# A PSUM bank for VectorE's score tiles, zero products in TensorE's gaps, and the later tiles' Q deferred

## The chip, the cores and the metric

The kernel runs on one core of a Trainium2 chip. The metric is the device time of one execution in microseconds (us). All numbers below are medians of several executions unless a single profiled one is named.

## The reference, cut to what matters

Two blocks, each an attention layer and a feed-forward layer (FFN), on 2048 positions of width 512, in bf16. There are 32 heads of only 16 columns, so the score matrix has 32 x 2048 x 2048 entries for each attention layer, and each needs an exponential.

```python
def _A_ref(x, wqkv, wo):
    H = 32; Dh = D // H                      # B, S, D = 1, 2048, 512
    qkv = ((x @ wqkv).reshape(B, S, 3, H, Dh)).transpose(2, 0, 3, 1, 4)
    q, k, v = qkv[0], qkv[1], qkv[2]
    p = softmax(einsum("bhqd,bhkd->bhqk", q, k) * Dh ** -0.5)
    o = einsum("bhqk,bhkd->bhqd", p, v)
    return o.transpose(0, 2, 1, 3).reshape(B, S, D) @ wo
def _B_ref(x, w1, b1, w2, b2):
    return gelu(_layernorm(x) @ w1 + b1) @ w2 + b2       # 512 -> 1376 -> 512
x = x + _A_ref(_layernorm(x), ...);  x = x + _B_ref(x, ...)      # twice
```

(The first lines are condensed; the layer norm inside `_B_ref` has no weights.)

## The kernel before

Scores are made in tiles of 128 keys x 512 queries of one head: 4096 tiles in all, each filling one of the eight PSUM banks (`ps` is declared as 128 x 8 x 512 floats). ScalarE takes the exponential of most tiles, two or three banks in one instruction. VectorE takes some (448 before) by an arithmetic of its own: it copies the tile out as integers (`dt`), and then four instructions on a pair of tiles make the exponential (`de`). TensorE then multiplies the result by V into bank 6.

The order of each engine's instructions is fixed in advance. The program plays the run through with a duration written beside every instruction, takes on each engine the task with the best priority among those ready, and emits the instructions in that order. So these durations do not set the time on the chip, but they decide who stands behind whom, and which tiles VectorE gets (it takes one if the plan says it is nearly idle).

```python
while pos < len(seq):                              # flow_scores: all tiles, in order
    ...
    G = 3 if wide else 2                           # 2 only in the first part of layer 1
    grp = seq[pos:pos + G]
    ...
    r = gi % 2
    b0 = G * r                                     # banks 0-2, then 3-5, in turn
    yield ("keys", [... ("free", last[b]) ...])    # both readers must have finished
    pt = yield ("get", "pt")
    dpos = self.choose_d(grp)                      # 0: VectorE gets the first tile; None: it gets none
    ops = []                                       # the group's score products
    ...
    yield Task("pe", 0.0, ops)
    ...                                            # one exponential on the other 2 or 3 banks:
    S_.submit(Task("act", ..., [I(lambda e, ...: e.activation(out=self.PT[:, pt, k0:k0 + n, :],
              in_=self.ps[:, b0 + k0:b0 + k0 + n, :], func=ACTF.Exp, scale=EXPS), ..., 0.085 + 0.4267 * n)]), cb=...)
    if dpos is not None:                           # VectorE drains its bank of the same group
        S_.submit(Task("dve", 0.0, [I(lambda e, ...: e.tensor_scalar(out=self.dt32[...],
                  in0=self.ps[:, b, :], ...), [("ps", b)], [("dt", ds, w)], 0.61)]), cb=...)
```

Layer 1 (the first attention layer) starts on little data: its first 512 queries meet the first 512 keys ("first part"), and later the other 1536 keys ("second part"), which can begin when K and V of the other twelve tiles of 128 positions are there. For each tile one job does the layer norm, a transposing DMA (`xnT`), the projections to K, Q and V, the copies out of PSUM, and the stores.

```python
def job_qkv_tile(self, L, tt, slot, i, left, prio):
    xr = yield ("get", "xn")                       # 3 slots; held until the transpose has landed
    yield self.ln_apply(tt, slot, i, xnr, ("xn", xr), prio)
    xs = yield ("get", "xnT")
    yield self.dma(lambda e: e.dma_start_transpose(self.xnT[:, xs, :, :], xnr), ...)
    ...                                            # mm(1): K, mm(0): Q, mm(2): V; four products each
```

At the end of each part, VectorE turns a row of Q into a column to put the two parts together (`rowT`).

## Time and profile before

| | before |
|---|---|
| time, median of 3 (lowest, highest) | 2046.51 us (2046.08, 2049.51) |
| span of the profiled execution | 2049.5 us |
| ScalarE busy, of it in 1387 exponentials | 1760.0 us, 1690.9 us |
| ScalarE idle just before exponentials | 207.3 us |
| of it from 53 to 205 us, and later | 73.1 us, 134.2 us |
| mean clock granted to TensorE | 0.689 |

To read it: ScalarE's work sets the time, so its idle time before exponentials is what a change can win. The main lines stand in the prediction. Three more views are needed afterwards for comparison. First the score products in the costliest groups (busy, mean ns of one, idle before them and what ended it):

```profile
L849 PE MATMUL ps<-QT,KT 32*128 32x512 bf16 x4096 | 738.0, 515 | 231.9 <-ACT PT L862 215.4 <-ACT dw L1019 5.2 <-DVE QT L792 4.6
```

Next the table of waits of TensorE's weight loads (total us, times, longest): score products that stood until VectorE had drained its tile.

```profile
PEld ps L849 <- DVE dt L874: 47.2, 134, 1.3
```

And the two longest unbroken runs of exponentials in the chain that ended last, from 1300 us on (start, us, what):

```profile
1427.91 11.40 ACT PT L862 x9
...
1836.59 11.78 ACT PT L862 x9
```

A product takes 515 ns in the mean.

### The profile page before, as it was taken

The numbers are of one execution on the slowest core, as the hardware profiler recorded it, in microseconds if no ns is written. First come the engines' busy times: TensorE is split into PE (matmuls) and PEld (weight loads), VectorE is DVE, ScalarE is ACT, GpSimd is POOL, SyncE is SP. The second block draws the span as 40 slices with busy tenths as digits, with TensorE's granted clock in tenths as the row PEclk, the third lists the DMA queues.
The fourth block names the chain that finished last, engine by engine and source line by source line (L and its number), as shares of the span: only waits on it lengthen the run. The fifth ranks groups of instructions, "written<-read, shape, count | busy, mean of one in ns | idle before, by whom it ended". The sixth has DMA issues, their size and how long they took to land.

```text
span 2049.5 us, 24833 instructions
## 1 busy us (share of the span) xinstructions
PE 1622.3 (79%) x9544; PEld 387.5 (19%) x9544; DVE 1543.8 (75%) x2378; ACT 1760.0 (86%) x1452; POOL 111.0 (5%) x230
## 2 busy tenths in 40 slices
PE   2877888887888878878788777787788788887886
PEld 1211111221111211222112211122112221122112
DVE  4657656888789788879777875698788787797882
ACT  1744999897999889989899879999999899999992
POOL 4110000001100020000200010000000000000000
PEclk9775555896667775688658885579556875588557
DMA  7782000101000010001511142100000000000000
GB/s 186 91 83 42 17 11 14 16 3 47 25 5 16 21 50 6 16 3 27 118 29 21 12 50 37 30 16 14 6 6 10 9 17 6 6 16 14 1 1 21
DMA packets 177957, 57.33 MB, mean 28 GB/s; under 512 B 160593, under 2 KB 171698, under 8 KB 177842
## 3 DMA queue, kind: packets, MB, share of 16 engines
q1 hardware_dynamic: 177842, 55.74, 15.2%
q8 instruction: 79, 1.29, 0.3%
q14 instruction: 36, 0.29, 0.1%
HBM read 10.92 MB, written 17.53 MB: 14 GB/s over the span
## 4 chain that ended last, share of the span: by engine, by line
ACT 40%; PE 34%; DVE 17%; DMA 5%; issue 2%; POOL 2%; SPq 0%; POOLq 0%; DVEq 0%
ACT PT L862 37%; PE ps L849 12%; PE ps L968 9%; PE ps L685 4%; DVE dt L874 3%; PE ps L1080 3%; PE ps L1114 3%; PE ps L1048 3%; DVE de L927 2%; DMA xnT<-xn 2%; DVE accT L998 2%; ACT h L1107 2%; DVE h L1100 1%; DVE de L930 1%; DVE dv L928 1%
## 5 line engine op out<-in xcount | busy, mean ns | idle before, releaser
L862 ACT ACTIVATE PT<-ps 128x1536 bf16<-128x1536 f32 (+1 forms) x1387 | 1690.9, 1308 | 207.3 <-PE ps L849 198.0
L849 PE MATMUL ps<-QT,KT 32*128 32x512 bf16 x4096 | 738.0, 515 | 231.9 <-ACT PT L862 215.4
L968 PE MATMUL ps<-PT,V 128*17 128x512 bf16 x3648 | 570.2, 515 | 38.4 <-DVE accT L998 19.7
L874 DVE TENSOR_SCALAR dt<-ps 128x512 int32<-128x512 f32 x448 | 299.9, 682 | 258.7 <-PE ps L849 257.6
L849 PEld LDWEIGHTS ps<-QT,KT 32*128 32x128 bf16 x4096 | 167.6, 96 | 835.4 <-PE ps L849 446.1
L927 DVE SCALAR_TENSOR_TENSOR de<-dt 128x1024 bf16<-128x1024 uint16 x226 | 270.2, 1199 | 1.4
L930 DVE SCALAR_TENSOR_TENSOR de<-dt,dv 128x1024 uint16<-128x1024 int32 x226 | 269.2, 1206 | 1.5
L685 PE MATMUL ps<-wqkv,xnT 128*128 128x512 bf16 x384 | 135.8, 475 | 72.7 <-DMA xnT<-xn 46.4
L968 PEld LDWEIGHTS ps<-PT,V 128*17 128x17 bf16 x3648 | 105.4, 89 | 406.0 <-issue 302.3
L968 PE MATMUL ps<-de,V 128*17 128x512 bf16 x448 | 140.9, 525 | 19.0 <-DVE de L930 19.0
L929 DVE TENSOR_TENSOR dv<-de,dv 128x1024 f16<-128x1024 bf16 x226 | 149.5, 675 | 0.2
L928 DVE TENSOR_SCALAR dv<-dt 128x1024 bf16<-128x1024 uint16 x226 | 149.4, 675 | 0.0
L1080 PE MATMUL ps<-yT,w 128*128 128x512 bf16 (+1 forms) x352 | 108.3, 421 | 25.0 <-DMA yT<-xn 13.2
L1114 PE MATMUL ps<-w,h 128*128 128x512 bf16 x280 | 86.8, 436 | 20.3 <-ACT g L1108 16.6
L998 DVE STREAM_TRANSPOSE accT<-ps 128x512 f32<-128x512 f32 x80 | 56.7, 708 | 55.8 <-PE ps L968 55.7
L637 POOL TENSOR_SCALAR rs<-mv 128x4 f32<-128x4 f32 (+1 forms) x19 | 11.6, 611 | 1601.6 <-DVE mv L630 1601.3
L1048 PE MATMUL ps<-wo,OT 128*128 128x512 bf16 x256 | 77.2, 422 | 3.3 <-DVE xres L1050 2.6
L1100 DVE TENSOR_SCALAR h<-ps,b1c 128x512 f32<-128x512 f32 (+1 forms) x77 | 56.7, 736 | 12.6 <-PE ps L1080 12.2
L685 PEld LDWEIGHTS ps<-wqkv,xnT 128*128 128x128 bf16 x384 | 31.1, 108 | 141.7 <-issue 73.9
L1031 DVE STREAM_TRANSPOSE OT<-ob 128x512 bf16<-128x512 bf16 x64 | 45.0, 702 | 0.3
L629 DVE BATCH_NORM_STATS2 st<-xres 128x6 f32<-128x512 bf16 x64 | 42.5, 669 | 0.0
L1080 PEld LDWEIGHTS ps<-yT,w 128*128 128x128 bf16 (+1 forms) x352 | 27.7, 104 | 76.4 <-issue 35.6
(94 smaller groups left out, 610.5 us busy)
## 6 DMA issues: line engine op xcount, KB each, us to landing
q_scr<-qk SPq DMA_DIRECT2D x22, 256.0 KB, 2.1
k_scr<-qk SPq DMA_DIRECT2D x12, 256.0 KB, 2.0
q_scr<-h SPq DMA_DIRECT2D x10, 256.0 KB, 3.8
m_scr<-accT SPq DMA_DIRECT2D x16, 136.0 KB, 9.2
MA<-m_scr SPq DMA_DIRECT2D x16, 136.0 KB, 2.2
out_dram<-xres SPq DMA_DIRECT2D x16, 128.0 KB, 1.7
v_scr<-vst SPq DMA_DIRECT2D x12, 136.0 KB, 1.7
V<-v_scr SPq DMA_DIRECT2D x8, 204.0 KB, 4.6
```

The source lines that it names most:

```text
L685: yield Task("pe", prio, [I(lambda e, c=c: e.matmul(self.ps[:, b, :], lhsT=self.xnT[:, xs, c, :], rhs=self.wqkv[:, c, which * 512:which * ...
L849: ops.append(I(lambda e, hp=hp, hg=hg, kb=kb, q=q, b=b: e.matmul(self.ps[:, b, :], lhsT=self.KT[32 * hp:32 * hp + 32, hg, kb * 128:(kb + 1 ...
L862: S_.submit(Task("act", 0.0 + 1e-5 * gi, [I(lambda e, pt=pt, k0=k0, n=n, b0=b0: e.activation(out=self.PT[:, pt, k0:k0 + n, :], in_=self.ps ...
L874: S_.submit(Task("dve", 0.0, [I(lambda e, ds=ds, w=w, b=b: e.tensor_scalar(out=self.dt32[:, ds, w * 512:(w + 1) * 512], in0=self.ps[:, b, ...
L927: yield Task("dve", pr, [I(lambda e: e.scalar_tensor_tensor(out=E, in0=lo, scalar=65536.0, in1=lo, op0=ALU.subtract, op1=ALU.mult), RT, [( ...
L928: yield Task("dve", pr, [I(lambda e: e.tensor_scalar(out=v, in0=lo, scalar1=CUB_B * sc / 65536.0, scalar2=CUB_A * sc, op0=ALU.mult, op1=AL ...
L929: yield Task("dve", pr, [I(lambda e: e.tensor_tensor(out=D, in0=E, in1=v, op=ALU.mult), [("de", es), ("dv", s)], [("dv", s)], 0.06 + 0.521 ...
L930: yield Task("dve", pr, [I(lambda e: e.scalar_tensor_tensor(out=Pb, in0=t32, scalar=2.0 ** -9, in1=D, op0=ALU.mult, op1=ALU.subtract), RT ...
L968: ops.append(I(lambda e, hp=hp, hg=hg, kb=kb, ap=ap, first=first: e.matmul(self.ps[32 * hp:32 * hp + 17, ACCB, :], lhsT=self.V[:, hg, kb, ...
L1048: yield Task("pe", pr, [I(lambda e, hg=hg, i=i, b=b: e.matmul(self.ps[:, b, :], lhsT=self.OT[:, hg, i * 128:(i + 1) * 128], rhs=self.wo[:, ...
L1080: yield Task("pe", pr, [I(lambda e, c=c: e.matmul(self.ps[0:M, b, :], lhsT=self.w1[:, c, fc * 128:fc * 128 + M], rhs=self.yT[:, c, :], sta ...
L1114: yield Task("pe", pr, [I(lambda e, fc=fc, i=i, b=b: e.matmul(self.ps[:, b, :], lhsT=self.gt(fc, i), rhs=self.w2[:, fc, :], start=(fc == 0 ...
```

## The change

Its intent has three parts. VectorE's tiles get bank 5 for themselves, and ScalarE works on groups of three tiles (banks 0 to 2) and two (banks 3 and 4) in turn, so that no group waits for two readers. Where the plan sees TensorE idle for more than 0.35 us, products with a zero matrix are put in, to keep its clock up; they add zero to bank 6, or write zeros to bank 7 while it is free. And Q of the later twelve tiles is left out at the start and made when K and V are done. With it the planned durations were set anew, and on-chip memory was found for a thirteenth slot of `PT` and the zero matrix: `rowT` lost its own buffer and takes one of the three `xn` slots. The new layout brought smaller rules with it: VectorE may take a tile from the next head group too, it stops 16 tiles before the end of a head group instead of 14, and value products wait for fewer ready tiles (5 instead of 9).

```diff
+            if t.eng == "pe" and self.filler is not None:      # in the scheduler
+                gap = pick[0] - self.P.free["pe"]
+                if gap > FILL_GAP:                             # 0.35
+                    self.filler(gap)
...
+    def fill_pe(self, gap):
+        n = int(FILL_F * (gap - 0.15) / FILL_T)                # 0.8, 0.11
+        ...
+        for _ in range(n):
+            P.op("pe", lambda e: e.matmul(self.ps[:, b, 0:FILL_N], lhsT=self.zw[:, :], rhs=self.wqkv[:, 0, 0:FILL_N], start=st, stop=st, skip_group_check=True), ...)
...
-            G = 3 if wide else 2
+            if wide:
+                b0, G = ((0, 3), (3, 2))[gi % 2]
+            else:
+                b0, G = ((0, 2), (2, 2))[gi % 2]
...
+            dt = self.take_d() if wide else None               # a tile for VectorE, into bank DLANE = 5
...
-        self.PT = t("PT", [128, PT_GROUPS, 3, 512], BF16)
+        self.PT = t("PT", [128, 13, 512], BF16)
-        self.rowT = t("rowT", [128, 512], BF16)
...
-            yield Task("dve", 1.2, [I(lambda e: e.transpose(self.rowT[:, :], self.QT[:, q, :]), [("qt", q)], [("rowT",)], 0.6)])
+            xs = yield ("get", "xn")
+            RX = ("xn", xs)
+            yield Task("dve", 1.2, [I(lambda e: e.transpose(self.xn[:, xs, :], self.QT[:, q, :]), [("qt", q)], [RX], 0.68)])
...
+        if later is not None:                                  # job_lnqkv: first "kv", then "q"
+            yield ("keys", [("n2k", L, tt) for tt in range(self.NT)])
+            for i, tt in enumerate(tiles):
+                self.S_.spawn(self.job_qkv_tile(L, tt, slot, i, left, later + 0.01 * i, "q"), later + 0.01 * i)
...
+LAT_PE = 0.20                                                  # planned: from a product to its reader (0.13 before)
...                                                            # and most planned durations, such as:
-  [("ps", b)], [("dt", ds, w)], 0.61)
+  [("ps", DLANE)], [("dt", ds, w)], 0.66)
```

In the program's order this makes 701 exponentials of three tiles, 764 of two and one of one, against 874 and 513; 464 tiles for VectorE against 448; and 3574 zero products.

## The prediction

> **What bounds the kernel now.** I read first the table of busy shares and the strip of slices, then the costliest groups, then the waits of ScalarE stretch by stretch, then a timeline of one plain attention stretch.
>
> ```profile
> PE 1622.3 (79%) x9544; PEld 387.5 (19%) x9544; DVE 1543.8 (75%) x2378; ACT 1760.0 (86%) x1452; POOL 111.0 (5%) x230
> ...
> ACT  1744999897999889989899879999999899999992
> ...
> PEclk9775555896667775688658885579556875588557
> ...
> L862 ACT ACTIVATE PT<-ps 128x1536 bf16<-128x1536 f32 (+1 forms) x1387 | 1690.9, 1308 | 207.3 <-PE ps L849 198.0
> ```
>
> ScalarE sets the time. It is busy 1760 us, nearly all of it in the 1387 exponentials, and the third number of the last line is the point: 207.3 us of idle stand just before those exponentials, of which 198.0 end when a score product lands. The rest of the 2049.5 us is a head (the first exponential starts at 53.3 us) and a tail (the last one starts at 2001.2 us). So with the same ScalarE work the most that can be won is about 207 us. PE's 79% is no bound: a product waiting in the pipe counts as busy. The clock row shows that TensorE is at half clock for long stretches.
>
> Where do the 207 us lie? The same ScalarE groups, by shape, in three stretches (each block is headed by its columns in the view; busy and mean of one, then idle before):
>
> ```profile
> L862 ACT ACTIVATE PT<-ps 128x1024 bf16<-128x1024 f32 x75 | 73.9, 1024 | 72.4 <-PE ps L849 71.6
> ...
> L862 ACT ACTIVATE PT<-ps 128x1536 bf16<-128x1536 f32 x368 | 505.1, 1467 | 26.3 <-PE ps L849 25.1
> L862 ACT ACTIVATE PT<-ps 128x1024 bf16<-128x1024 f32 x197 | 198.0, 1033 | 49.3 <-PE ps L849 46.8
> ...
> L862 ACT ACTIVATE PT<-ps 128x1536 bf16<-128x1536 f32 x333 | 455.2, 1465 | 14.5 <-PE ps L849 13.4
> L862 ACT ACTIVATE PT<-ps 128x1024 bf16<-128x1024 f32 x192 | 192.4, 1038 | 23.8 <-PE ps L849 20.8
> ```
>
> The first line is 53 to 205 us (start of layer 1), the next two 350 to 1150, the last two 1300 to 2001. The start alone loses 73 us. In the two long stretches the short exponentials (two tiles, because VectorE took the third) lose 49.3/197 = 0.25 and 23.8/192 = 0.12 us each, the long ones only 26.3/368 = 0.07 and 14.5/333 = 0.04. The remaining 21 us are 3.6 between 205 and 350 and 17 at the change of layers (1150 to 1300). So the mixed groups are what hurts, as the change supposes.
>
> ```profile
> 53.00:205.00 152.00, 117.61 (x524) 25.70 (x520) 95.32 (x185) 87.14 (x85) 21.73 (x67) 0.66 0.64 71
> ...
> 1440.00:1550.00 110.00, 54.20 (x264) 11.56 (x261) 0.50 0.03 6
> ...
> 1478.21 0.14 PEld L849 LDWEIGHTS ps<-QT,KT 32*128 32x128 bf16 x3 [0.67 <-PE ps L849]
> 1478.24 0.61 PE L849 MATMUL ps<-QT,KT 32*128 32x512 bf16 x3 [0.19 <-ACT PT L862]
> ```
>
> The first line is the start in the table of stretches: ScalarE busy 87 of 152 us, DMA share 0.64, no engine full; it is a chain of transfers, projections and evictions. The second is the score products in a stretch without projections: 264 of them and a clock of exactly 0.50. The last two show a refill there: three products take 0.61 us at half clock and wait for ScalarE to leave the banks.
>
> **What the Trainium skill says.** "TensorE: Matmul & The Clock Gate", Part 1: the array runs at half clock unless the last activity window of about 3.4 us was busy, and the granted ratio is binary. The trace agrees (0.50 held for whole stretches) and adds something: score and value products, which use 32-row or 32-column tiles, do not count enough. Between 1440 and 1550 us PE is issuing all the time and stays at 0.50, while stretches with full 128x128 projections reach 0.75 to 0.93. "PSUM — Partial Sum Buffer", section on bank collisions: two engines may not touch one bank and quadrant together, so a bank goes back to TensorE only when its reader has finished; here the three banks of a group go back only when both ScalarE and VectorE are done. "TensorEngine Tiling (Array Packing)", Key Properties: changing the tiling mode drains TensorE. The trace shows 0.23 us of weight-load wait at warm switches, so fillers (full mode) between tiled products are not free. "ScalarE: Activation LUTs", What ACT_TABLE_LOAD costs: back-to-back activations overlap by some 93 ns. Here two of 1024 take 1.94 us and one 1.03, so 0.92 each; eleven of 1536 take 14.77 in the chain of waits and one 1.45, so 1.33 each.
>
> **The change part by part.** Counts are from the built programs' instruction order.
>
> ScalarE work. Before: 874 long and 513 short exponentials, 874 x 1.33 + 513 x 0.92 = 1634 us. After: 701 long, 764 short and one of a single tile (0.5): 932 + 703 + 1 = 1636 us. Gelu and table loads are the same. VectorE takes 464 tiles in place of 448, which just pays for the 79 extra instructions. Net +2 us: the change does not unload ScalarE, it can only remove idle.
>
> VectorE's own bank. Before, after a short exponential ScalarE has only 0.92 us of cover while TensorE refills three banks, one of which VectorE has first to drain (0.68 us, and it may stand behind a 1.2 us instruction). After, ScalarE's groups wait for ScalarE alone. But the cover alternates for good: the two-bank group is refilled under 1.33 us, the three-bank group under 0.92 us, some 690 times. A refill is a release of about 0.19 us, products of 0.61 (cold) or 0.39 (warm), and about 0.1 to the start of the activation: 0.9 cold, 0.68 warm. Cold it has no slack; warm it has 0.24 us. So this part needs the next one.
>
> Zero products. 3574 products of 256 columns in some 760 bursts. By columns they equal 1787 full products; TensorE has 1344 of its own. Counted along the order, every run of 64 scores has at least 31 full-product equivalents, or at least 3.6 per 3.4 us at 7.5 scores per window. Laying the clock record over the products before, windows that stayed warm had mostly 3 or more full ones (mean 5.7) and windows that stayed cold 0.4. So I expect the clock at 0.9 or above from 60 us on. Their cost: at full clock 256 columns are half of the 0.215 us seen for a warm 512-column projection, so 3574 x 0.107 = 382 us plus 760 switches x 0.1 = 76. The other PE work when warm: 1466 score groups x 0.32 = 469, some 1200 value groups x 0.32 = 384, 1344 x 0.215 = 289 and switches about 50. Sum 1650 us in 1950: it fits, but PE has little slack, and a burst placed wrongly holds a score group by up to some 0.5 us.
>
> Mid-kernel sum. Idle before exponentials from 205 to 2001 us is 134 now. After: in stretches without projections, half of the 690 cycles, warm slack of 0.24 us leaves perhaps 0.02 each (7 us); in stretches with projection and FFN pairs of 0.53 us, which cannot be interrupted, I take the 0.12 us that warm three-tile groups after two short ones wait now (345 x 0.12 = 41); layer change 15. About 65. Gain 134 - 65 = 69 us.
>
> Early Q deferred. For 12 tiles, Q projection (4 products at 0.43, 20 us in all when cold), a VectorE eviction, half of the square and its sum and one small operation (0.69 + 0.34 + 0.6 + 0.18, 22 us in all) and the 256 KB store (landing about 4 us in this stretch) leave the start; later 12 more normalisations (0.40 each) and 12 input transposes come back at low priority, where the DMA share is 0.06. The first part of layer 1 has 64 short exponentials: 64 x 0.92 = 59, so it could end at 112 us, but the second part starts at 179 because K and V of 12 tiles are late. The load of that stretch falls by roughly a quarter on PE, VectorE and DMA, so 118 us (60 to 178) become about 88. Gain about 30 us, leaving some 43 of the 73.
>
> Sum: 2046.5 + 2 - 69 - 30 = 1950 us, after rounding.
>
> **The rivals.** (a) PE becomes the bound: the fillers run late, or the clock stays cold and each takes 0.21 us. Against it: cold overfull PE is itself activity that warms the clock, and the sum above leaves 300 us. For it: an order fixed in advance, and every score group sits behind whatever is in front. It would leave mid idle near 134 or above, time 1990 to 2060. (b) The start is bound by transposes, which stay (KT and xnT land in about 5.4 us, DMA share 0.77 to 0.80 in slices up to 150): deferral gains 10 rather than 30, time 1970. (c) VectorE becomes the bound: 28 half batches instead of 4 and 16 more tiles add about 50 us to 1544, so 82% of 1950; in FFN stretches it is at 88% now. Time 1970 to 1980. (d) Everything aligns: mid idle 30, start idle 25, time 1900.
>
> **Range and chances.** Main uncertainty is the mid term (gain 20 to 100) and the start (10 to 45), largely independent: 1905 to 2000 for 8 in 10. 2% is 41 us, that is below 2005.6; only rival (a) or two halved terms together miss it. Faster 0.88, within 0.11, slower 0.01.
>
> **What would show it.** Clock row at 8 to 9 nearly throughout; ScalarE busy within 20 us of 1760; idle before its exponentials near 110 instead of 207, with the long ones now waiting more than the short; second part of layer 1 starting near 150 instead of 179; no wait of scores on VectorE's drain of any size. Wrong if the clock stays near 0.7, if idle before exponentials remains above 170, or if score products are found standing behind zero products.

## The result, and the profile after

The changed kernel takes **1915.39 us** (median of 4, 1911.82 to 1917.96), a ratio of 0.9351 with a 95% interval of 0.9332 to 0.9370. Ratios here are the mean time of one kernel's runs over that of the other's runs of the same rounds, so they are not quite the ratio of the medians quoted. That is faster, inside the predicted range, and 35 us below the predicted 1950.

The page of the changed kernel: busy shares, the strip of the clock, and two of the costliest groups.

```profile
span 1913.1 us, 32397 instructions
...
PE 1743.7 (91%) x13118; PEld 671.1 (35%) x13118; DVE 1600.0 (84%) x2511; ACT 1734.6 (91%) x1531; POOL 122.2 (6%) x230
...
PEclk9989999999999999999999989999999999999999
...
L921 ACT ACTIVATE PT<-ps 128x1024 bf16<-128x1024 f32 (+1 forms) x1466 | 1666.1, 1293 | 100.4 <-PE ps L915 96.3
...
L853 PE MATMUL ps<-wqkv,zw 128*128 128x256 bf16 x3574 | 530.0, 277 | 0.0
```

The clock row is at 8 or 9 throughout, and the idle before exponentials is 100.4 us instead of 207.3. There are also 25 us less of busy time in them, though ScalarE has 79 more instructions to do; that is taken up below. By stretch (53 to 205 us, 350 to 1150, from 1300), as the prediction shows it of before:

```profile
L921 ACT ACTIVATE PT<-ps 128x1024 bf16<-128x1024 f32 x89 | 89.8, 1055 | 33.7 <-PE ps L915 33.3
...
L921 ACT ACTIVATE PT<-ps 128x1536 bf16<-128x1536 f32 x321 | 482.4, 1503 | 17.8 <-PE ps L915 16.2
L921 ACT ACTIVATE PT<-ps 128x1024 bf16<-128x1024 f32 x320 | 344.7, 1077 | 17.8 <-PE ps L915 17.5
...
L921 ACT ACTIVATE PT<-ps 128x1536 bf16<-128x1536 f32 x235 | 362.1, 1541 | 4.2 <-PE ps L915 3.0
L921 ACT ACTIVATE PT<-ps 128x1024 bf16<-128x1024 f32 x234 | 261.1, 1116 | 4.7 <-PE ps L915 4.6
```

The start loses 33.7 us (with 6.0 before long exponentials, 39.7) instead of 73.1. Long and short groups now wait alike: 0.06 us each in the middle, 0.02 in the last stretch. The table of stretches for 53 to 205 and 205 to 350 us (busy us and instructions of PE, PEld, DVE, ACT, POOL, then clock, DMA share, GB/s):

```profile
53.00:205.00 152.00, 128.09 (x863) 43.75 (x860) 110.86 (x218) 119.63 (x117) 17.84 (x27) 0.93 0.61 66
205.00:350.00 145.00, 129.76 (x1000) 49.58 (x999) 130.03 (x227) 133.17 (x123) 14.06 (x35) 0.96 0.12 32
```

At the start ScalarE is busy for 119.63 of 152 us instead of 87.14. The timeline of TensorE in a quiet stretch shows what the refills look like now:

```profile
1474.36 0.39 PE L915 MATMUL ps<-QT,KT 32*128 32x512 bf16 x3 [0.19 <-ACT PT L921]
1474.69 0.39 PE L1040 MATMUL ps<-PT,V 128*17 128x512 bf16 x4
...
1475.93 0.61 PE L853 MATMUL ps<-wqkv,zw 128*128 128x256 bf16 x4
1476.62 0.39 PE L915 MATMUL ps<-QT,KT 32*128 32x512 bf16 x3
```

Three score products take 0.39 us, where they took 0.61. The four zero products take 0.61 together, of which the first is 0.27, so about 0.11 for each further one, and the scores after them follow. Over the whole kernel the score products show the same (group list, with the idle before them):

```profile
L915 PE MATMUL ps<-QT,KT 32*128 32x512 bf16 x4096 | 600.3, 385 | 81.0 <-ACT PT L921 56.1 <-ACT dw L1090 1.3
```

And in the chain that ended last, from 1300 us on, ScalarE now carries it for 96 exponentials without a break, where nine were the most:

```profile
1330.71 108.59 ACT PT L921 x96
```

**Where 136.4 us came from** (2049.5 - 1913.1, the profiled spans): 33.4 from idle before exponentials up to 205 us (73.1 to 39.7), 73.5 from that idle later (134.2 to 60.7), 24.8 from the busy time in exponentials (1690.9 to 1666.1), and 4.7 from the rest.

### The profile page after: what moved, and what is told of

Same layout as the page of the kernel before. It is cut to its first block, busy times and chain, and to the rows that moved or that the text cites. A ratio compares the mean times of both kernels' runs of the same rounds, so it can differ in the third digit from the quotient of the medians. Undisturbed runs are those within 1.5% of the kernel's fastest.

```text
span 1913.1 us, 32397 instructions
## 1 busy us (share of the span) xinstructions
PE 1743.7 (91%) x13118; PEld 671.1 (35%) x13118; DVE 1600.0 (84%) x2511; ACT 1734.6 (91%) x1531; POOL 122.2 (6%) x230
## 4 chain that ended last, share of the span: by engine, by line
ACT 51%; PE 34%; DVE 6%; DMA 6%; POOL 1%; issue 1%; SPq 0%; POOLq 0%; DVEq 0%
ACT PT L921 48%; PE ps L915 10%; PE ps L1040 6%; PE ps L853 5%; PE ps L1153 4%; PE ps L1121 3%; PE ps L709 3%; PE ps L1187 3%; DMA xnT<-xn 2%; ACT h L1180 2%; DVE dt L932 1%; DMA yT<-xn 1%; DMA b1s<-in_B_b_dram 1%; DVE de L1002 1%; DMA MA<-m_scr 1%
## 5 line engine op out<-in xcount | busy, mean ns | idle before, releaser
L921 ACT ACTIVATE PT<-ps 128x1024 bf16<-128x1024 f32 (+1 forms) x1466 | 1666.1, 1293 | 100.4 <-PE ps L915 96.3
L915 PE MATMUL ps<-QT,KT 32*128 32x512 bf16 x4096 | 600.3, 385 | 81.0 <-ACT PT L921 56.1
L853 PE MATMUL ps<-wqkv,zw 128*128 128x256 bf16 x3574 | 530.0, 277 | 0.0
L1040 PE MATMUL ps<-PT,V 128*17 128x512 bf16 x3632 | 435.3, 387 | 10.5 <-DVE accT L1067 10.0
L853 PEld LDWEIGHTS ps<-wqkv,zw 128*128 128x128 bf16 x3574 | 298.9, 98 | 211.9 <-issue 175.6
L1002 DVE SCALAR_TENSOR_TENSOR de<-dt,dv 128x1024 uint16<-128x1024 int32 (+1 forms) x246 | 284.0, 1155 | 2.3
L999 DVE SCALAR_TENSOR_TENSOR de<-dt 128x1024 bf16<-128x1024 uint16 (+1 forms) x246 | 283.7, 1153 | 2.3
L709 PE MATMUL ps<-wqkv,xnT 128*128 128x512 bf16 x384 | 113.1, 405 | 54.9 <-DMA xnT<-xn 50.2
L1001 DVE TENSOR_TENSOR dv<-de,dv 128x1024 f16<-128x1024 bf16 (+1 forms) x246 | 159.7, 650 | 2.3
L1000 DVE TENSOR_SCALAR dv<-dt 128x1024 bf16<-128x1024 uint16 (+1 forms) x246 | 160.0, 651 | 0.0
L1153 PEld LDWEIGHTS ps<-yT,w 128*128 128x128 bf16 (+1 forms) x352 | 26.8, 102 | 52.3 <-issue 29.4
```

The costliest lines, as they stand in the source:

```text
L709: yield Task("pe", prio, [I(lambda e, c=c: e.matmul(self.ps[:, b, :], lhsT=self.xnT[:, xs, c, :], rhs=self.wqkv[:, c, which * 512:which * ...
L853: P.op("pe", lambda e: e.matmul(self.ps[:, b, 0:FILL_N], lhsT=self.zw[:, :], rhs=self.wqkv[:, 0, 0:FILL_N], start=st, stop=st, skip_group_ ...
L915: ops.append(I(lambda e, hp=hp, hg=hg, kb=kb, q=q, b=b: e.matmul(self.ps[:, b, :], lhsT=self.KT[32 * hp:32 * hp + 32, hg, kb * 128:(kb + 1 ...
L921: S_.submit(Task("act", 1e-5 * gi, [I(lambda e, pt=pt, n=n, b0=b0: e.activation(out=self.PT[:, pt:pt + n, :], in_=self.ps[:, b0:b0 + n, :] ...
L999: yield Task("dve", pr, [I(lambda e: e.scalar_tensor_tensor(out=E, in0=lo, scalar=65536.0, in1=lo, op0=ALU.subtract, op1=ALU.mult), RT, [( ...
L1000: yield Task("dve", pr, [I(lambda e: e.tensor_scalar(out=v, in0=lo, scalar1=CUB_B * sc / 65536.0, scalar2=CUB_A * sc, op0=ALU.mult, op1=AL ...
```

## The experiments

Twelve kernels. Each was correct against the reference, and each was compared with the kernel before on the same chip, where that took 2046.5 to 2053.2 us in the median. "Idle" is ScalarE's before exponentials; "start" is its part from 53 to 205 us.

The zero products, the deferred Q and the bank (with the re-set durations) can each be there or not, which makes eight kernels. With before and after, six experiments fill the table:

| ratio to before | without zero products | with zero products | what these do |
|---|---|---|---|
| neither bank nor deferred Q | 1 (before) | 0.9641 (b_fill) | -3.6% |
| deferred Q | 0.9798 (b_qdefer) | 0.9426 (b_fill_q) | -3.8% |
| bank and new durations | 0.9888 (a_laneonly) | 0.9411 (a_noqdefer) | -4.8% |
| all of these | 0.9803 (a_nofill) | 0.9351 (after) | -4.6% |

Read down a column, the deferral is worth 2.0 and 2.2% without the bank, 0.9 and 0.6% with it; the bank is worth 1.1 and 2.4% without the deferral, with it nothing cold (0.9803 against 0.9798) and 0.8% warm. So the zero products bring something like the same everywhere, a little more with the bank, while bank and deferral take from each other.

### a_nofill: after, without zero products

```diff
-        S_.when([("qt", 0)], lambda: setattr(S_, "filler", self.fill_pe))
```

The order of everything else is the same instruction by instruction, since the filler only uses gaps of the plan.

> The changed kernel without its zero products; every other instruction stands in the same order. Theory C (the clock carries the gain: the three-bank refill has 0.92 us of cover and needs 0.9 us at half clock, 0.68 at full clock): clock back to 0.65 to 0.72, idle before the exponentials up from 100 to 180 to 250 us, time 1990 to 2060. Rival B (VectorE's own bank carries it, the zero products are ballast): clock low as well, but idle below 125 us and time 1905 to 1935.

Measured: 2010.92 us, ratio 0.9803 (0.9776 to 0.9831), mean clock 0.703. Its clock row and its two kinds of exponentials:

```profile
PEclk9775665797678875788658866578557865578558
...
L921 ACT ACTIVATE PT<-ps 128x1536 bf16<-128x1536 f32 x701 | 1020.3, 1455 | 76.8 <-PE ps L915 72.0
L921 ACT ACTIVATE PT<-ps 128x1024 bf16<-128x1024 f32 x764 | 782.4, 1028 | 94.7 <-PE ps L915 90.6
```

Idle is 171.5 us against 100.4 with zero products, a little under the 180 that I had expected at least. So in this order 4.6% of the time hangs on adding products that compute nothing.

### a_filltiled: the same zero products on a strip of 32 rows

```diff
-  lhsT=self.zw[:, :], rhs=self.wqkv[:, 0, 0:FILL_N], ...
+  lhsT=self.zw[0:32, :], rhs=self.wqkv[0:32, 0, 0:FILL_N], ..., tile_position=(0, 0)
```

It asks whether the zero products help by themselves or by the clock.

> The same 3574 zero products in the same places, but on one 32-row strip of the array instead of all 128 rows. Theory C, with the reading that strip products do not count as activity: the clock stays near 0.65 to 0.75 and each zero product costs twice as much, so time 2020 to 2150, above the run without any. Rival (what the zero products do is keep TensorE's queue moving, whatever rows they use, or strip products do count): clock 0.95 or above, time 1910 to 1935.

Measured: 2242.68 us, ratio 1.0915 (1.0872 to 1.0957), mean clock 0.689, just that of before. The clock row, the long exponentials, and the duration of the zero products (lowest, median, highest ns, in the view of their line):

```profile
PEclk9765555888567975887567875677557855677557
...
L921 ACT ACTIVATE PT<-ps 128x1536 bf16<-128x1536 f32 x701 | 1022.6, 1459 | 244.4 <-PE ps L915 238.3 <-PE ps L853 1.4
...
L853 PE MATMUL ps<-wqkv,zw x3574: 265/416/417, 49.7 to 2220.4; 32*128 32x256 bf16 x199
```

As many products in the same places, and the clock does not move. In the cold they take 416 ns where the full ones take 273, the bursts planned for full speed overrun their gaps, and the scores stand behind them: the long exponentials' idle rises from 76.8 to 244.4 us, and the zero products make 21% of the chain that ended last. So the gain of the zero products is the clock, and without it they are a loss of 232 us, which is more than I had expected (2020 to 2150 us in all). The run changes the rows used and the tiling form at once, so which of these the clock looks at is not told apart.

### b_fill: before, with zero products

```diff
+    def fill_pe(self, gap): ...        # as in the change, with its call, constants and zero matrix
-        self.ioi = t("ioi", [128, 128], F32)
+        self.ioi = self.h32[:, 10, 0:128]      # room for the zero matrix, as in the change
```

> The kernel before with zero products alone (4242 of them by the same rule; groups of three with VectorE's tile inside). If the clock alone carries the gain: idle before the exponentials near 120 us, time 1950 to 1970. If bank and clock are both needed: short exponentials still wait for VectorE's drain, warm gaps were 0.2 us after a short one already, so idle 150 to 180 us, time 1990 to 2020.

Measured: 1981.00 us, ratio 0.9641 (0.9619 to 0.9662), clock 0.973. The exponentials over the whole run, then the short ones from 53 to 205 us:

```profile
L892 ACT ACTIVATE PT<-ps 128x1536 bf16<-128x1536 f32 x874 | 1193.0, 1472 | 27.0 <-PE ps L879 26.1
L892 ACT ACTIVATE PT<-ps 128x1024 bf16<-128x1024 f32 x513 | 506.4, 1062 | 126.7 <-PE ps L879 125.4
...
L892 ACT ACTIVATE PT<-ps 128x1024 bf16<-128x1024 f32 x71 | 70.4, 1031 | 81.4 <-PE ps L879 81.0
```

Idle is 153.7 us: 81.4 at the start, which a faster clock does not help, and 72.3 after it, where before has 134.2. Mixed groups are still there, with VectorE's tile among ScalarE's, and its waits with them (table of waits):

```profile
PEld ps L879 <- DVE dt L904: 27.4, 96, 0.8
```

So 62 us of the later idle go with the clock alone, of the 69 that the prediction expected from bank and zero products together, while the groups stay mixed. The time falls between my two expectations: neither "the clock alone" (1950 to 1970) nor "both needed" (1990 to 2020).

### b_qdefer: before, with Q deferred

```diff
-    ... self.job_lnqkv(1, list(range(4 * ck, 4 * ck + 4)), 1.8 + 0.1 * ck)
+    ... self.job_lnqkv(1, list(range(4 * ck, 4 * ck + 4)), 1.8 + 0.1 * ck, 2.6 + 0.1 * ck)
     # with job_lnqkv and job_qkv_tile of the change
```

> The kernel before with Q of the last 12 tiles deferred, nothing else. My prediction had 30 us for it; undoing it in the changed kernel cost 16. If the start is held by transfers and evictions whatever the clock, this gains 15 to 30 us (2020 to 2035) and idle of ScalarE between 53 and 205 us falls from 73 to 40 to 50. If the deferred work comes back as new waits in the next stretch, the start gains about 30 and the whole 5 to 15 (2035 to 2045).

Measured: 2011.45 us, ratio 0.9798 (0.9780 to 0.9815), clock 0.708. The exponentials from 53 to 205 us:

```profile
L878 ACT ACTIVATE PT<-ps 128x1024 bf16<-128x1024 f32 x77 | 75.2, 1027 | 38.8 <-PE ps L865 38.2
L878 ACT ACTIVATE PT<-ps 128x1536 bf16<-128x1536 f32 x32 | 43.9, 1460 | 3.1 <-PE ps L865 3.1
```

Start idle is 41.9 us instead of 73.1, so 31.2 less; the whole gain in the medians against before (2053.21) is 41.8, more than either of my expectations. The other 10.8 us are idle after the start (123.4 us instead of 134.2); why that fell is not shown.

### a_noqdefer and a_laneonly: after without the deferral, and without the zero products too

```diff
-    ... self.job_lnqkv(1, ..., 1.8 + 0.1 * ck, 2.6 + 0.1 * ck)
+    ... self.job_lnqkv(1, ..., 1.8 + 0.1 * ck)
```

> The changed kernel with Q made at once for all tiles, as before. My theory: the start is held by the chain of transfers and evictions, so it loses about 30 us: time 1935 to 1955, idle of ScalarE between 53 and 205 us back above 60. Rival: the warm clock and not the deferral shortened the start, time 1912 to 1925.

> The bank for VectorE, the groups of 3 and 2 and the re-fitted planning durations alone: no zero products, Q made early. The run without zero products but with deferred Q gave a ratio of 0.980; if the parts add, Q deferral is worth 0.006 to 0.01 of that, so this run comes at 0.986 to 0.99, 2020 to 2035 us. If Q deferral carries all of it at half clock, it comes at 0.998 to 1.005, since the three-bank refill at half clock (0.9 us against 0.92 of cover) loses what the drained bank wins.

Measured: a_noqdefer 1931.78 us (3 us under the range that I expected), ratio 0.9411 (0.9392 to 0.9429), clock 0.981, idle 122.9, of it 73.8 at the start and 49.1 after it. a_laneonly 2031.75 us, ratio 0.9888 (0.9863 to 0.9913), clock 0.692, idle 198.5. The bank with its durations is therefore worth 1.1% cold and 2.4% warm (0.9411 over 0.9641) where Q is not deferred. That agrees with the prediction's view that the bank needs the clock, and its size is below what the prediction led one to think.

After has 34 us less idle at the start than a_noqdefer, yet the time differs by 16. The gain is lost again soon after the start, as this table shows (worked out from the traces: the us at which the exponential starts that brings ScalarE's tiles to the given share):

```
share      before  b_qdefer  b_fill  b_fill_q  a_noqdefer   after  a_rowown
0.04        187.7     154.3   197.2     148.6       188.7   152.3     156.4
0.06        222.0     190.5   230.4     182.7       221.7   185.2     189.3
0.10        290.1     259.8   297.4     250.3       287.6   266.0     256.4
0.12        324.8     293.4   331.4     283.4       320.3   297.6     288.3
0.50       1060.8    1014.7  1032.7     975.5       989.6   973.8     966.8
0.999      1999.8    1958.0  1931.6    1877.5      1884.8  1864.6    1853.8
```

At shares of 0.04 and 0.06 after leads a_noqdefer by 36 us, at 0.10 by 22. In the kernel before, the deferral keeps its lead: b_qdefer is 33 us ahead at 0.04 and 31 at 0.12. So something in after takes back some 15 us between the shares 0.06 and 0.10, that is between 185 and 266 us of its run. (The expectation below says 19: it was read from an earlier count of this table, which did not stop at the same share in every kernel.) The timeline there has this, a transfer with three issues and then VectorE:

```profile
244.02 4.71 SPq L684 DMA_TRANSPOSE xnT<-xn  x3
...
248.19 0.71 DVE L1076 STREAM_TRANSPOSE xn<-QT 128x512 bf16<-128x512 bf16 x1 [3.77 <-DMA xnT<-xn]
```

VectorE wants to turn the row of Q at the end of a head group, the row now goes to an `xn` slot, and the slot is still being read by the transposing DMA of a deferred Q tile. It stands still for 3.77 us, with everything in line behind it. The whole run has four such waits, 11.6 us (table of waits):

```profile
DVE xn L1076 <- DMA xnT<-xn: 11.6, 4, 4.9
```

### a_rowown: after, with a place of its own for the row

```diff
-            xs = yield ("get", "xn")
-            RX = ("xn", xs)
+            own = L == 1
+            if own:      # a slice of the FFN's buffer, which is not in use yet
+                RX, rt = ("h", 5), self.h32[:, 10, 0:256].bitcast(BF16)
+            else:
+                xs = yield ("get", "xn")
+                RX, rt = ("xn", xs), self.xn[:, xs, :]
```

> The changed kernel, in which the transposed Q row of layer 1 has a place of its own again (a slice of the FFN buffer that is idle then) instead of a slot of the three-slot normalised-input buffer. My theory: in the changed kernel VectorE stands up to 4.9 us behind an input-transpose transfer that still reads the slot, and this is how 19 us of the deferral's 34 are given back between 6 and 10 per cent of the tiles: the wait of the row transpose on a transfer falls from 11.6 us to below 3, idle of ScalarE between 205 and 350 us from 11.8 to 2 to 6, time down 6 to 15 us, ratio 0.928 to 0.932. Rival (the deferred Q's own VectorE and TensorE work takes the time back): the wait goes and the time stays, ratio 0.934 to 0.937.

Measured: **1904.86 us**, ratio 0.9308 (0.9287 to 0.9330), clock 0.982; it beats both kernels, after by 10.5 us in the medians. From 205 to 350 us, after first:

```profile
L921 ACT ACTIVATE PT<-ps 128x1536 bf16<-128x1536 f32 x59 | 89.5, 1518 | 6.2 <-PE ps L915 6.1
L921 ACT ACTIVATE PT<-ps 128x1024 bf16<-128x1024 f32 x58 | 63.5, 1096 | 5.6 <-PE ps L915 5.6
```

```profile
L921 ACT ACTIVATE PT<-ps 128x1536 bf16<-128x1536 f32 x64 | 98.9, 1545 | 1.8 <-PE ps L915 1.7
L921 ACT ACTIVATE PT<-ps 128x1024 bf16<-128x1024 f32 x63 | 70.8, 1123 | 0.0
```

The 11.8 us of idle in this stretch become 1.8, and 127 exponentials are made instead of 117. VectorE's wait of 11.6 us for the transfer is gone. In the table of shares a_rowown is 4.1 us behind after at 0.06, 9.3 ahead at 0.12 and 10.8 at the end: the gain arises here and is kept. Its lead over a_noqdefer is 32 us at 0.06 and still 32 at 0.12, so what after lost in this stretch goes with the shared slot. Over the whole run a_rowown beats a_noqdefer by 1.1% (0.9308 over 0.9411), which is still less than the 2.0 to 2.2% that the deferral is worth without the bank. That rest stays open: in a_noqdefer the row shares the slot too (4.0 us of such waits), and a kernel without deferral and with its own row was not run.

### b_fill_q: before, with zero products and deferred Q

The edits of b_fill and b_qdefer together, nothing else.

> The kernel before with zero products and deferred Q, but VectorE's tile still inside the group of three and the durations of before: the missing corner. If the parts simply multiply (0.9641 x 0.9798), the ratio is 0.945, 1938 us, and the bank adds 1 per cent to that in the full change. If zero products and deferral overlap (both shorten the start), 0.955 or above, and the bank is worth 2 per cent or more.

Measured: 1927.27 us, ratio 0.9426 (0.9398 to 0.9455), clock 0.986, idle 99.0, of it 33.6 at the start. Two of the three parts make 5.7% of the 6.5%, and the two add up nearly as their product (0.9641 x 0.9798 = 0.9446). Clock and idle (100.4 in after) are as in after, and the start is 6 us better, without any bank for VectorE; the 12 us by which after leads lie almost all in the busy time of the exponentials, 1677.0 us here and 1666.1 there. Most of that is overlap lost to short waits that make no idle: 83 exponentials here start so late that they add more than 1.00 us (two tiles) or 1.36 (three) in a row, 16 in after (counted in the traces; on this overlap see below). The chain that ended last shows the bank's part as well: VectorE has 17% of it in before, 21% here and 6% in after. The 0.8% is a low figure for the bank, since here the row of Q has its own buffer and in after it shares a slot; a_rowown against b_fill_q gives 1.2% (0.9308 over 0.9426).

### a_olddur and b_newdur: the planned durations changed over

```diff
-LAT_PE = 0.20                      # a_olddur; b_newdur is the reverse, in before
+LAT_PE = 0.13
-  [("ps", DLANE)], [("dt", ds, w)], 0.66)
+  [("ps", DLANE)], [("dt", ds, w)], 0.61)
   # and so for all that the change re-set
```

> The changed kernel planned with the durations and the one cross-engine latency of before. The plan is more optimistic about VectorE and gives it 506 tiles in place of 464, so ScalarE has 42 tiles less, 42 x 0.41 = 17 us. Theory R (the re-fit is a part of the gain, because zero products are placed by planned gaps): zero products and score groups collide, VectorE falls behind, 1930 to 1970 us. Rival (the re-fit is decoration): 1895 to 1915 us, faster by the tiles it moved.

> The kernel before planned with the new durations, nothing else. The plan gives VectorE 433 tiles in place of 448, so ScalarE has 15 more, 6 us. Rival to the bank (the better plan, not the bank, removed the waits): idle before the exponentials falls by 20 us or more, 2025 to 2035 us. My theory: no better than before, 2045 to 2060 us, idle within 15 of 207.

Measured: a_olddur 1936.26 us, ratio 0.9429 (0.9409 to 0.9448); VectorE takes 506 tiles in its plan instead of 464. b_newdur 2058.97 us, ratio 1.0026 (1.0011 to 1.0041), with 433 tiles instead of 448. So the new durations are worth nothing in the kernel before, and with the old ones the bank is worth nothing beside the zero products and the deferral (0.9429 against 0.9426 of b_fill_q). Only together do they give the last 0.8%. What a_olddur lacks points to VectorE; its page says of the chain that ended last:

```profile
DVE 43%; PE 31%; ACT 13%; DMA 7%; issue 3%; POOL 2%; SPq 1%; POOLq 0%; DVEq 0%
```

In after VectorE has 6% of that chain. So with 506 tiles, planned on shorter durations, VectorE is the engine that is waited for, the prediction's rival (c). How much of that is the number of tiles and how much the order is not shown.

### a_fill06: a quarter fewer zero products

```diff
-FILL_F = 0.8
+FILL_F = 0.6
```

> The changed kernel with zero products in 0.6 of each planned gap instead of 0.8: 2637 of them, 26 per cent fewer, which leaves about 2.7 full-product equivalents in 3.4 us where it was 3.6. If the clock follows a threshold near 3 as read from the clock record, it falls back in the attention stretches: mean 0.75 to 0.92, time 1930 to 1970. If there is room, the clock stays above 0.95 and score products wait less behind zero products: time 1900 to 1915.

Measured: 1913.12 us, ratio 0.9353 (0.9325 to 0.9381), 2637 zero products instead of 3574, clock 0.971 in the profiled execution and up to 0.978 in the others. The time is that of after. The clock has room: 26% fewer products still keep it nearly up, and fewer of them do not help, so if the zero products hold up the scores, it is by no more than the slightly lower clock costs. The clock record goes in steps of 3.41 us. Counting in each the products on all rows and columns, in units of 512 columns, here a step with 2 to 3 of them was followed by one at full clock in 83 of 90 cases, one with 1 to 2 in 4 of 10, and one with less than 1 in 0 of 7 (in before 10 of 22 with 2 to 3). How few would do was not sought.

### a_rowown_tail12: more tiles for VectorE

```diff
-DTAIL = 16      # VectorE takes no tile of a head group once fewer than this are left in it
+DTAIL = 12
```

> The version with the own place for the transposed row, in which VectorE may also take tiles until 12 are left of a head group (16 before): the plan gives it 477 tiles in place of 464. If ScalarE's work still sets the time, 13 tiles x 0.41 = 5 us less and a ratio of 0.926 to 0.930 against 0.931. If VectorE (84 per cent busy) is by now the partner that ends a head group, its later tiles hold up the end of each group and with it the next value products: idle before the exponentials rises by 10 us or more and the ratio is 0.932 to 0.940.

Measured: 1927.10 us, ratio 0.9390 (0.9368 to 0.9412), clock 0.980, 477 tiles for VectorE. It is level with a_rowown until 55% of the tiles and loses some 20 us between 55 and 70%, at the change of layers; the ends of head groups, where the edit acts, are spread over the whole run. The chain that ended last, in that stretch:

```profile
1121.95 9.86 DMA q_scr<-qk
...
1131.94 0.70 DVE qk L715
...
1132.69 1.03 PE ps L709 x2
```

A store of Q that lands in 2.0 us in the median takes 9.86 here, VectorE's next copy into that buffer waits 5.9 us for it, and a projection that TensorE has next in its fixed order waits for the copy. ScalarE's waits from 1072 to 1370 us are, in this kernel and then in a_rowown:

```profile
ACT PT L921 <- PE ps L915: 33.8, 23, 6.3
```

```profile
ACT PT L921 <- PE ps L915: 14.4, 16, 2.1
```

So a new plan moved a transfer and its reader together at one place. The ratio falls into the second range that I expected, but by luck: the cause named there, VectorE at the ends of head groups, is not where the time goes. The run says little of how many tiles VectorE should take: any edit of the plan shifts the order everywhere.

## Why the prediction was right or wrong

**The bound and the ceiling.** ScalarE's idle was what could be won, as predicted: 106.9 of the 136.4 us are that idle, which fell from 207.3 to 100.4 (predicted near 110).

**The clock.** Predicted 0.9 or above; measured 0.983, and 0.93 already in the first stretch. The reading that score and value products do not keep it up is confirmed: the 3574 products on a 32-row strip left 0.689 with TensorE 94% busy. The threshold of about three full products in a window was too careful: in a_fill06 two to three were enough in 83 of 90 cases.

**The cost of zero products.** Their step of 0.107 us is 0.11 in the timeline. TensorE is busy 1743.7 us, more than the 1650 summed (the zero products alone 530.0 against 382 + 76), and it is still no bound, since the time did not fall with 26% fewer of them. One sign of being wrong did show, score products behind zero products: these have 5% of the chain that ended last in after. In a_fill06 they have 2%, at the same time. Rival (a), TensorE as the bound, fell in this kernel. a_filltiled shows it was a real one: with the clock down the same bursts cost 232 us against none at all. The argument held against it, that an overfull cold TensorE warms its own clock, did not hold there; with products on all rows no run tests it. The 0.23 us of weight-load wait, read as a price of switches, is not one: TensorE is still busy with the products before. The 0.1 us per switch in the sum fits the timelines better (0.33 us from three score products to the value products after them, where one full product of that length takes 0.216).

**The middle.** Predicted 134 to 65, measured 134.2 to 60.7: the size is right, but partly by luck, because the cause was put wrongly. The prediction held mixed groups to be "what hurts" and gave the bank the first place, with the zero products as its helper. b_fill, with mixed groups, has 72.3. The clock is the larger cause and works alone; the bank brings 0.8 to 2.4% beside the zero products, and beside both other parts nothing without the new durations. The prediction's own sum could have warned me: it gave a cold refill 0.9 us against a cover of 0.92, no slack, and a warm one 0.68, whichever engine reads the bank.

**Long and short.** "Long ones now waiting more than the short" is wrong: from 205 us on, 29.6 us before long ones and 31 before short ones, in about 675 of each. The slack of 0.24 us that the prediction worked out for the warm refill was enough more often than it thought.

**The start.** Predicted 30 us, leaving 43; measured 33.4, leaving 39.7. The second part of layer 1 starts at 144.5 us instead of 179.5 (predicted near 150). The deferral does it: b_qdefer has 41.9, and a_noqdefer still 73.8. Rival (b), transposes as the bound, fell. But not all of it reached the end: deferral is worth 2.0% in before and only 0.6% in after (0.9351 over 0.9411). The prediction let Q come back "at low priority, where the DMA share is 0.06" and saw no price in it. A price was the `xn` slot that the row of Q shares with those transposes: without it, in a_rowown, the kernel is 10 us faster. The rest of the difference stays open.

**VectorE.** Predicted 82% busy, measured 84%; as the time lies well below the 1970 of rival (c), VectorE did not become the bound. The waits of scores on its drain (47.2 us) are gone from the table of waits, as predicted.

**The term that was mis-sized.** The sum had "ScalarE work: net +2 us". It counted the back-to-back time, 1634 and 1636 us, and so took the busy time as fixed ("within 20 us of 1760"; it is 1734.6). But an exponential that starts after a gap adds its whole length, 1.02 us for two tiles and 1.45 for three in the median, and one in a row adds only 0.92 and 1.34, in before and after alike (counted in both traces). In before 389 exponentials began after a gap or a table load, in after 190, and 199 x 0.107 = 21 us of the 24.8. Another 2 us are the work in a row: with 0.916 and 1.343 us it comes to 1643.7 us before and 1641.7 after. And an exponential that starts just before the one in front of it ends loses part of the overlap without any idle. That explains b_fill, where the gaps fall to 214, which makes 19 us, and the busy time fell by only 13.5: there 85 exponentials in a row add more than 1.00 or 1.36 us, in before 17. The prediction quoted that very overlap, used it for the work, and left it out of the price of a wait: each gap avoided saves its idle and about 0.1 us more. With 21 us in place of +2 it would have said 1927.

The account closes in spans: 136.4 measured less 96.5 predicted is 39.9, of which 26.8 are this term (24.8 and the 2 with the wrong sign), 4.5 the middle, 3.4 the start, and 4.7 what the sum did not have; the last half us is rounding. In medians the miss is 34.6, mostly because the profiled execution of before (2051.24 us) was 4.7 us slower than the median that the prediction started from. Of the two other rivals, (d) with idle of 30 later and 25 at the start went further than the runs did (60.7 and 39.7), though its 1900 us is near the 1904.86 of a_rowown, by way of the busy time.

## What to carry to other kernels

When an engine waits hundreds of times for short refills, look at the clock row first: here work that computes nothing, on all 128 rows and only in planned gaps, bought 3.6 to 4.8%, while the rebuilt bank layout bought at most 2.4% and needed its plan re-fitted. Count a wait on a pipelined engine as its idle and the overlap that it breaks. And when work is moved to a later place, check which buffers it holds there: a slot shared with a slow transfer took back about a third of what the deferral had won at the start.

## What the Trainium skill lacked or had wrong

- "TensorE: Matmul & The Clock Gate", Part 1, says that a busy window raises the clock; apart from transposes, which Part 4 sets apart, the page does not say which products count as busy. Here 8192 score and value products in tiled form, with 3574 more zero products on 32 rows, left the mean at 0.689. The same number on 128 rows, zeros too, gave 0.983, and 2637 of them 0.971.
- "ScalarE: Activation LUTs", What ACT_TABLE_LOAD costs, has the overlap of back-to-back activations (93 ns; here 0.107 us, from 1.024 and 0.917 for two tiles) and not what follows from it: with 199 fewer gaps, ScalarE's busy time in exponentials fell by 24.8 us at nearly equal work.
- "TensorEngine Tiling (Array Packing)", Key Properties, says that a change of tiling mode drains the array and gives no figure. In the timelines three score products and the value products after them start 0.54 us apart at half clock (before, 1474.21 and 1474.75 us) and 0.33 at full clock (after, 1474.36 and 1474.69), some 0.11 more than the 0.427 and 0.216 us between two full products of 512 columns in a row. That this is the drain is not shown.
